# One more block of an MLP by fewer products: seven for block one's down projection, eleven for block two's up projection, with the weights' sums moved between engines

## The chip, the core and the metric

The kernel runs on one core of a Trainium2 chip. A core has five engines that work beside each other, each through its own queue in order: PE (TensorE, matrix products; the profile lists its weight loads apart as PEld), DVE (VectorE), ACT (ScalarE), POOL (GpSimd) and SP (SyncE, which issues most of the DMAs here). They meet only through semaphores. The metric is the time of one execution on the device in microseconds. Three executions before the change took 661.83, 662.26 and 664.05 us; the median is 662.26.

## What is computed

Two stages in float32. The first is a delta-rule attention over 4 batches, 8 heads, 768 tokens and head size 48. The second is an MLP over its output, 3072 tokens of 384 features, with 2048 hidden features. `_attn_ref` gets its shapes from q, k, v of (4, 8, 768, 48).

```python
for t in range(S):
    kt, vt, bt = (k_n[:, :, t], v[:, :, t], beta[:, :, t, None])
    y[:, :, t] = np.einsum('bhd,bhde->bhe', q[:, :, t], state)
    v_old = np.einsum('bhde,bhd->bhe', state, kt)
    state = state + bt[:, :, :, None] * np.einsum('bhd,bhe->bhde', kt, vt - v_old)
...
h = x @ w_in                       # x: (3072, 384), w_in: (384, 2048)
relu6 = np.clip(h + 3.0, 0.0, 6.0)
g = h * relu6 / 6.0
return (g @ w_out).astype(np.float32)   # w_out: (2048, 384)
```

`k_n` is k divided by its norm.

## The kernel before the change

**Tiling.** The 768 tokens are cut into 24 steps `t` of 32 tokens; with 4 batches one step is 128 rows. Two steps make a block of 256 rows, so the MLP has 12 blocks. The attention of a step is a chain of small products on PE: `sc` (scores, L547), `ks` (state times keys and queries, L806), `pz` (the inverse X times R, L827), `su` (the update of the state, L938), `py` and the transposition `yt`. X comes from an inverse of 32x32 triangles, done for a group of four steps at once: a transposition (L469), some sixty short steps on DVE that take turns (L759 multiplies into `pr`, L764 subtracts from `A`), and a transposition back (L473). The group that holds steps 5 to 8 is called `i2` in the order.

**The MLP of a block.** The up projection makes `ph`, ACT and DVE turn it into `g` (the hardswish), and the down projection multiplies `g` with `w_out` into `po`. There are two forms of each:

- the plain up projection `up` (L994): for each of 16 chunks f three products of 128x256, then ACT's relu (L1001) and a DVE step (L1004) that reads `ph` and so releases its place in PSUM;
- `up_by_eleven`: the product as blocks of 2 by 2 with sums taken on both sides. It needs sums of `w_in` (`S1`, `S2`, `S4` and a changed `W21`, made by `weight_sums` on POOL at L1030, 16 operations of 128x256), sums of the tokens (`token_sums`, DVE L1056), and per pair of chunks two sums on POOL (L1030), two on DVE (L1093, L1097), ACT's L1080, L1100 and L1110 and DVE's L1113;
- the plain down projection `down` (L1162): for each of the two steps 16 products of 128x384, then an eviction on ACT (L1173) and a DMA;
- `down_by_seven` (L1226): seven products of halves, 8 matmuls of 128x192 each. It needs sums of `w_out` (`T1`, `T2`, `T4`, and a changed quarter `B12`), made by `quarters` (L1197, 12 operations of 128x384 on DVE) and `last_quarter` (L1203, 4 more), and per block eight sums of `g` on DVE (L1212), five copies on ACT (L1233) and seven adds of results on POOL and DVE (L1236).

`FIRST = 2` says that block two's down projection is the first by seven, `UF = 3` that block three's up projection is the first by eleven. Blocks zero and one are plain, and so is block two's up projection.

**Where things lie.** `T1`, `T2` and `T4` live in the three parts of `spare`. Parts 0 and 1 hold raw data of weight pieces before they are converted, part 2 holds scratch of the conversion. The conversion of a piece is three steps on DVE (L378, L383, L389, the word `c` in the order) and four on ACT (L356, the word `a`). The last piece, number 15, lies raw in part 1. `S1`, `S2`, `S4` live in `sums_in`, which serves as scratch of the attention early on. All small products share PSUM: `po`, `ph`, `pt`, `py`, `yt` and `pz` take turns in four places (the ring `pm`), `sc`, `ks` and `su` in two (the ring `pc`). A place is taken again when its reader on DVE or ACT is done.

**What sets the order.** The first part of the program is written out by hand in `ORDER`: each word emits the next unit of one of several generators (`u` a unit of the MLP, `ru` a relu, `gu` the DVE step L1004, `i2` a step of the second inverse, `h4`, `y4`, `p8` and so on the attention's). `mlp_units` interleaves block zero's down projection with block one's up projection, 32 units of `u`, and then goes on to block one's down projection, four units of which are in `ORDER`. From step 5 on a loop of 15 units for each step takes over: it takes the attention's parts at fixed units (`plan`), one unit of the MLP, one of `rest` (the conversion, then `quarters`), and fills in the next inverse. `weight_sums` is taken two operations to a unit in block two's down projection. Each engine runs its instructions in the order in which they are emitted, and waits at each for what it needs.

## Time and profile before

| What | Value |
|---|---|
| executions | 661.83, 662.26, 664.05 us (median 662.26) |
| profiled execution: span from first to last instruction | 660.3 us |
| median less span | 2.0 us; no other time of the profiled execution is listed |
| granted TensorE clock, mean | 0.997 |
| block zero's down with block one's up projection | about 94 to 151 us |
| block one's down projection, plain | about 148 to 179 us |
| block two's up projection, plain | 178.8 to 205.9 us |
| block two's down projection, by seven | 205.9 to 230.2 us |
| block three's up projection, by eleven | 230.2 to 255.9 us |
| token step 5: `pz` on PE | 160.96 us |

How to read it: the profile has a row for each engine with its busy time; PE's matmuls overlap by pipelining, so the distance from one piece of the chain to the next is a better measure of PE work than the time of one record. Each fp32 matmul of the program appears as two records. A timeline row gives start, duration, engine, line, output and inputs; in brackets the idle time ahead of it and what ended it. A windows row gives the length of a stretch, the busy time of PE, PEld, DVE, ACT and POOL with the number of instructions, the granted clock and the DMA share with its rate. Line numbers are those of the kernel before.

### The profile page before, as it was taken

What the parts mean: (1) busy time and instruction counts of PE and PEld (TensorE: products, weight loads), DVE (VectorE), ACT (ScalarE), POOL (GpSimd) and SP (SyncE); (2) the same over time, 40 slices, a digit from 0 to 9 for tenths busy, and PEclk for the clock granted to TensorE, in tenths of its full rate; (3) what the DMA queues carried; (4) which work ended last, traced back from release to release, by engine and by line L of the source; (5) the groups of instructions that cost most, each with busy time, mean ns of one, the idle gap of its engine ahead of it and who ended that gap; (6) DMA issues with size and microseconds to landing.
All of it is one profiled execution on the core that took longest, in us unless ns stands there. A gap on an engine that the chain in (4) does not pass through costs nothing.

```text
span 660.3 us, 26640 instructions
## 1 busy us (share of the span) xinstructions
PE 632.5 (96%) x11640; PEld 569.2 (86%) x11640; DVE 499.2 (76%) x1170; ACT 282.3 (43%) x548; POOL 225.1 (34%) x352
## 2 busy tenths in 40 slices
PE   2768999999999999999999999999999999999997
PEld 2658987776689989999999999999999999999997
DVE  5899877798657988758988848979658998456354
ACT  5887689332243154154154244244244144153250
POOL 6531022003661353553254354164051242331430
PEclk9998999999999999999999999999999999999999
DMA  7888346202040030041030030020020020000000
GB/s 174 204 198 235 77 102 164 51 25 43 9 87 18 3 74 3 3 90 22 3 74 3 2 74 3 2 63 2 3 50 2 3 49 3 23 18 2 26 1 24
DMA packets 88692, 33.28 MB, mean 50 GB/s; under 512 B 80224, under 2 KB 83424, under 8 KB 88576
## 3 DMA queue, kind: packets, MB, share of 16 engines
q1 hardware_dynamic: 88224, 31.29, 20.8%
q8 instruction: 91, 1.49, 0.9%
q10 hardware_dynamic: 352, 0.30, 0.2%
q14 instruction: 25, 0.20, 0.1%
HBM read 26.84 MB, written 4.72 MB: 48 GB/s over the span
## 4 chain that ended last, share of the span: by engine, by line
PE 91%; DVE 3%; DMA 2%; SPq 1%; ACT 1%; issue 1%; DVEq 0%
PE po L1226 28%; PE ph L1066 27%; PE ph L994 9%; PE po L1162 6%; PE ks L806 4%; PE su L938 3%; PE pt L524 3%; PE pz L827 3%; PE py L827 3%; PE sc L547 2%; PE yt L873 1%; DMA spare<-in_moe_w_in_dram 1%; PE pi L684 1%; DMA w_out<-in_moe_w_in_dram 1%; SPq L168 1%
## 5 line engine op out<-in xcount | busy, mean ns | idle before, releaser
L1066 PE MATMUL ph<-xT,w_in 128*128 128x128 f32 (+1 forms) x720 | 156.8, 321 | 0.0
L1030 POOL TENSOR_TENSOR g<-g 128x256 f32<-128x256 f32 (+1 forms) x144 | 88.6, 616 | 104.7 <-ACT g L1080 99.1
L1066 PEld LDWEIGHTS ph<-xT,w_in 128*128 128x128 f32 x720 | 116.8, 191 | 6.7
L1226 PE MATMUL po<-w_out,g 128*128 128x192 f32 x640 | 110.6, 326 | 0.0
L1226 PEld LDWEIGHTS po<-w_out,g 128*128 128x128 f32 x640 | 104.6, 190 | 0.5
L1080 ACT ACTIVATE g<-ph 128x512 f32<-128x512 f32 x72 | 43.1, 598 | 105.1 <-PE ph L1066 105.1
L1226 PE MATMUL po<-spare,g 128*128 128x192 f32 x480 | 86.7, 332 | 0.0
L1226 PEld LDWEIGHTS po<-spare,g 128*128 128x128 f32 x480 | 77.2, 190 | 1.8
L994 PE MATMUL ph<-xT,w_in 128*128 128x128 f32 (+1 forms) x384 | 72.0, 338 | 0.6 <-ACT xT L877 0.6
L1236 POOL TENSOR_TENSOR o<-o,u 128x192 f32<-128x192 f32 x18 | 13.3, 739 | 163.8 <-ACT o L1233 86.6
L994 PEld LDWEIGHTS ph<-xT,w_in 128*128 128x128 f32 x384 | 59.6, 195 | 7.7 <-ACT xT L877 0.8
L1093 DVE TENSOR_TENSOR g<-ph,g 128x256 f32<-128x256 f32 x72 | 30.2, 419 | 46.8 <-PE ph L1066 33.5
L759 DVE TENSOR_TENSOR pr<-A 128x30 f32<-128x30 f32 (+9 forms) x150 | 57.3, 382 | 3.3
L1212 DVE TENSOR_TENSOR g<-g 128x512 f32<-128x512 f32 x80 | 56.1, 722 | 3.5 <-PE po L1226 3.5
L1113 DVE SCALAR_TENSOR_TENSOR g<-o,g 128x512 f32<-128x512 f32 x72 | 52.6, 730 | 7.8 <-ACT o L1110 7.7
L764 DVE TENSOR_TENSOR A<-A,pr 128x30 f32<-128x30 f32 (+9 forms) x150 | 55.1, 367 | 3.3
L1110 ACT ACTIVATE o<-g,halves 128x512 f32<-128x512 f32 x72 | 52.2, 725 | 11.3 <-DVE g L1113 8.4
L1066 PE MATMUL ph<-beta_tok,sums_in 128*128 128x128 f32 x288 | 55.9, 275 | 0.0
L356 ACT ACTIVATE spare<-spare,places 128x768 uint16<-128x768 uint16 (+1 forms) x56 | 52.8, 947 | 3.2 <-DMA kf<-in_k_dram 1.6
L1233 ACT ACTIVATE o<-po 128x192 f32<-128x192 f32 x40 | 13.3, 332 | 82.7 <-PE po L1226 79.2
L510 POOL TENSOR_TENSOR kb<-kf,inv 128x384 f32<-128x384 f32 x24 | 21.7, 907 | 75.5 <-issue 43.1
L1162 PE MATMUL po<-w_out,g 128*128 128x384 f32 x128 | 45.4, 490 | 0.0
(141 smaller groups left out, 1019.1 us busy)
## 6 DMA issues: line engine op xcount, KB each, us to landing
kf<-in_k_dram SPq DMA_DIRECT2D x96, 48.0 KB, 2.6
qb<-in_q_dram SPq DMA_DIRECT2D x96, 48.0 KB, 2.4
vf<-in_v_dram SPq DMA_DIRECT2D x96, 48.0 KB, 2.1
out_dram<-o SPq DMA_DIRECT2D x90, 48.0 KB, 1.6
spare<-in_moe_w_in_dram SPq DMA_DIRECT2D x4, 768.0 KB, 6.6
w_out<-in_moe_w_in_dram SPq DMA_DIRECT2D x4, 768.0 KB, 6.1
w_out<-in_moe_w_out_dram SPq DMA_DIRECT2D x4, 768.0 KB, 5.8
spare<-in_moe_w_out_dram SPq DMA_DIRECT2D x4, 768.0 KB, 5.2
```

Source lines behind the costliest of these rows:

```text
L356: nc.scalar.activation(out=z, in_=z if n else d.bitcast(I16)[:, :, :, 3], func=func, bias=places[:, n : n + 1], scale=scale,)
L759: nc.vector.tensor_tensor(out=pv, in0=A[:, j + 1 :, j].unsqueeze(2).to_broadcast([n, w, j]), in1=A[:, j, 0:j].unsqueeze(1).to_broadcast([n ...
L764: nc.vector.tensor_tensor(out=A[:, j + 1 :, 0:j], in0=A[:, j + 1 :, 0:j], in1=pv, op=ALU.subtract)
L994: nc.tensor.matmul(ph[:, cols], lhsT=w_in[:, s, f * 128 : (f + 1) * 128], rhs=xT[:, s, cols], start=(s == 0), stop=(s == NKT - 1),)
L1030: nc.gpsimd.tensor_tensor(out=out, in0=a, in1=b, op=op)
L1066: nc.tensor.matmul(ph[:, n], lhsT=w, rhs=x, start=start, stop=stop, skip_group_check=True)
L1080: nc.scalar.activation(out=gt, in_=ph[:], func=ACTF.Copy)
L1110: nc.scalar.activation(out=r, in_=g, func=ACTF.Relu, bias=half, scale=1.0 / 6.0)
L1113: nc.vector.scalar_tensor_tensor(out=g, in0=r, scalar=1.0, in1=g, op0=ALU.min, op1=ALU.mult)
L1162: nc.tensor.matmul(pos[c][:], lhsT=gs[blk, f // 2][:, f % 2, c * P : (c + 1) * P], rhs=w_out[:, f, :], start=(f == 0), stop=(f == NFC - 1),)
L1212: nc.vector.tensor_tensor(out=A(f, *out, 4), in0=A(f, *a, 4), in1=A(f, *b, 4), op=op)
L1226: nc.tensor.matmul(ps[n][:], lhsT=A(f - f % 2, *a)[:, f % 2], rhs=b[:, f], start=(f == 0), stop=(f == HF - 1),)
```

## The change

Four things change together.

1. `FIRST` goes from 2 to 1: block one's down projection is by seven products. For this block product 2 is done in four parts: two ahead of product 4, two behind it, and ahead of product 4 the program asserts that the sums of `w_out` and all hidden features are there. `settle()` at the start is left out for it.
2. `quarters` makes all sixteen sums of `w_out`, now on POOL, and `last_quarter` is gone. They are emitted by a new word `T` of the order, sixteen times, between the units of block zero's down and block one's up projection. The four that overwrite `B12` come last, behind block zero's products that read it. The second and third converting step of the last weight piece and its last step on ACT are emitted earlier, so that they stand ahead of the sums that read them.
3. `UF` goes from 3 to 2: block two's up projection is by eleven. `weight_sums` is taken in block one, one operation to a unit of its down projection (sixteen units) instead of two to a unit in block two's.
4. `rest` is the conversion alone, and the special cases for plain blocks behind block zero are gone.

```diff
 ORDER (its last lines)
-u h4 k*2 c q k*9 q u p8*2 x4 k ru k*2 gu k c n9 q u q*2 p8 k*2 b7 n9*2 i2 u x4 q i2*2 q ub ru gu u
-rb gb i2*2 h4*2 u*2 i2 ru i2*6 y4 i2 gu i2*7 u i2 ru gu i2 u*3 ru i2*4 gu ru i2*2 v i2 c gu u*3 a u
-ru c i2 u*2 i2 gu i2*3 q ...
+u h4 k*2 c q k*9 q u p8*2 x4 k ru k*2 gu k c a n9 q u T q*2 p8 k T k b7 n9 T n9 i2 c u T x4 q i2 c
+i2 q ub T ru gu u rb T gb i2*2 T h4*2 u T u i2 ru i2 T i2*4 T i2 y4 i2 gu T i2*4 T i2*3 u i2 T ru gu
+i2 u T u*2 ru i2*2 T i2*2 gu ru i2 T i2 v i2 gu u*4 ru i2 u*2 i2 gu i2*3 q ...
...
-    UF = 3
+    UF = 2
...
+        past.add(("down", c, f0))
...
-    FIRST = 2
+    FIRST = 1
...
     def quarters():
-        for o, a, b in ((T1, B12, B11), (T2, B22, T1), (T4, T2, B21)):
+        for o, a, b, hi in (
+            (T1, B12, B11, False), (T2, B22, T1, True), (T4, T2, B21, True), (B12, B22, B12, True),
+        ):
             for f in range(0, HF, 2):
-                nc.vector.tensor_tensor(
+                needs(("w", NWI + (f + HF * hi) // WF), ("w", NW - 2 + hi))
+                if o is B12:
+                    needs(("down", 0, f), ("down", 1, f))
+                nc.gpsimd.tensor_tensor(
                     out=o[:, f : f + 2], in0=a[:, f : f + 2], in1=b[:, f : f + 2], op=ALU.subtract
                 )
+                if o is B12 and f == HF - 2:
+                    past.add("quarters")
                 yield
-
-    def last_quarter(f):
-        nc.vector.tensor_tensor(
-            out=B12[:, f : f + 2], in0=B22[:, f : f + 2], in1=B12[:, f : f + 2], op=ALU.subtract
-        )
...
-        def product(n, a, b, half):
+        def product(n, a, b, part, parts=2):
...
-            for f in range(half * HF // 2, (half + 1) * HF // 2):
+            for f in range(part * HF // parts, (part + 1) * HF // parts):
...
-        settle()
+        if blk > FIRST:
+            settle()
         product(1, A11, B11, 0)
...
+        parts = 2
+        if blk == FIRST:
+            parts = 4
+            for part in range(2):
+                product(2, A12, B21, part, parts)
+                yield
+            needs("quarters", *(("read", ("ph", blk, f, None)) for f in range(NFC)))
         product(4, A22, T4, 0)
...
-        product(2, A12, B21, 0)
+        product(2, A12, B21, parts - 2, parts)
...
-        product(2, A12, B21, 1)
+        product(2, A12, B21, parts - 1, parts)
...
-            for _ in downs(blk):
-                next(sums, None)
+            for _ in down_by_seven(blk):
                 next(sums, None)
                 yield
             if blk + 1 < N // CB:
                 mode["of"] = "eleven" if blk + 1 >= UF else "up"
-                for n, _ in enumerate((up_by_eleven if blk + 1 >= UF else up)(blk + 1)):
-                    if blk + 1 == FIRST and n >= HF:
-                        drain(rest)
-                        if n % 2:
-                            last_quarter(n - HF - 1)
-                    yield
+                yield from (up_by_eleven if blk + 1 >= UF else up)(blk + 1)
...
-    rest = chained(convert(), quarters())
+    rest = convert()
...
-        ua=up(0, 0), ub=up(0, 1), u=mlp_units(),
+        ua=up(0, 0), ub=up(0, 1), u=mlp_units(), T=quarters(),
```

## The prediction

> **What bounds the kernel now.** I read the page's busy shares and its forty slices first, then the chain that ended last, then the windows between 94 and 256 us, and at last the timelines of VectorE (DVE) and GpSimd (POOL) in the stretch that the change touches.

> ```profile
> span 660.3 us, 26640 instructions
> PE 632.5 (96%) x11640; PEld 569.2 (86%) x11640; DVE 499.2 (76%) x1170; ACT 282.3 (43%) x548; POOL 225.1 (34%) x352
> PE   2768999999999999999999999999999999999997
> DVE  5899877798657988758988848979658998456354
> 119.00:154.00 35.00, 35.00 (x464) 25.35 (x464) 32.06 (x87) 9.86 (x22) 0.00 (x0) 1.00 0.21 43
> ```

> PE is full from 61 us to the end, so a microsecond of PE work is worth a microsecond wherever nothing else is late. The windows row (busy us of PE, PEld, DVE, ACT, POOL) shows something second: from 119 to 154 us DVE is busy for 32.06 of 35 us and POOL runs nothing. The next rows are of the chain, then of the timelines of DVE and of POOL.

> ```profile
> 154.80 1.49 PE po L1162 x4
> 205.86 2.60 PE po L1226 x16
> ```

> ```profile
> 124.07 1.95 DVE L469 STREAM_TRANSPOSE A<-L 128x1024 f32<-128x1024 f32 x1
> 127.44 0.25 DVE L759 TENSOR_TENSOR pr<-A 128x84 f32<-128x84 f32 x1
> 133.72 0.41 DVE L1004 SCALAR_TENSOR_TENSOR g<-g,ph 128x256 f32<-128x256 f32 x1
> 137.60 0.95 DVE L383 SCALAR_TENSOR_TENSOR spare<-spare 128x768 f32<-128x768 uint32 x1
> 159.10 0.60 DVE L909 SCALAR_TENSOR_TENSOR R<-ks,parity,R 128x384 f32<-128x384 f32 x1
> 173.03 2.35 DVE L1197 TENSOR_TENSOR spare<-spare,w_out 128x384 f32<-128x384 f32 x2
> 201.23 0.66 DVE L759 TENSOR_TENSOR pr<-A 128x84 f32<-128x84 f32 x1
> ```

> ```profile
> 154.89 0.83 POOL L510 TENSOR_TENSOR kb<-kf,inv 128x384 f32<-128x384 f32 x1 [43.06 <-issue]
> ...
> 173.03 0.83 POOL L498 TENSOR_TENSOR bkb<-kb,beta_tok 128x384 f32<-128x384 f32 x1
> 173.82 1.14 POOL L510 TENSOR_TENSOR kb<-kf,inv 128x384 f32<-128x384 f32 x1
> ...
> 201.06 0.73 POOL L1030 TENSOR_TENSOR sums_in<-sums_in,w_in 128x256 f32<-128x256 f32 x1
> 216.26 0.59 POOL L1236 TENSOR_TENSOR o<-o,u 128x192 f32<-128x192 f32 x1 [13.68 <-ACT o L1233]
> ```

> DVE shows no idle gap from 121.65 to 162.74: it runs the inverse of the second group (L469, then L759/L764 in turn), which token 5's pz needs together with R, finished at 159.70. PE starts that pz at 160.96, so this chain has 1.26 us to spare, and it has POOL silent beside it (43.06 us idle). That silence matters: the same L759 step takes 0.25 us at 127.44 and 0.66 at 201.23, where a POOL operation of 0.73 began 0.17 us earlier. At 173.03 two L1197 that take about 0.55 each alone take 2.35 beside two POOL operations, and the second of these takes 1.14 instead of 0.83. Each waits for the other in turn. Steps that read PSUM (L1004, L956) keep their time beside POOL.

> **The change, part by part.**

> *PE work.* Block one's product: 64 records of L1162, pieces of the chain 2.58+2.58+1.49+1.29+2.58+1.49+1.29+2.78+2.78+1.29+1.29 = 21.44 us. By seven it is 112 records like block two's, 2.60+1.50+1.30+2.60+5.40+2.80+2.60 = 18.80: -2.64. Block two's up projection: 96 records of L994, 4.08+1.49+1.30+2.59+5.38+2.79+3.89 = 21.52; by eleven like block three's, 3.38+1.09+1.54+2.43+2.62+2.62+2.62+3.96 = 20.26: -1.26. Together -3.90. Of the seven products three come before token 5's pz, where half of the old product stood, so PE would reach pz 2.6 us sooner; only the 1.26 lies behind it.

> *Sixteen sums from DVE to POOL in block zero.* DVE loses 12 L1197 and 4 L1203. Two of these stood before token 5's R (0.78 and 0.61 between starts): -1.39 there; one new L1212 takes their place, +0.60. In the built order the first T2 write needs the second converting step (L383) of the last weight piece to be done with that buffer; that step now stands behind the transpose, 124.07+1.95+0.95, about 127 us. The four T1 need only the piece before, and start near 115, beside PSUM steps and a 1.7 us gap: 0, at most 2 us. The other twelve, and the first four weight sums queued behind them (0.73 each), wait for nothing but their own queue, so sixteen POOL operations run from 127 on beside the L759/L764 chain.

> Price of one: POOL rows with two full inputs take 0.47 (128 columns), 0.59 (192), 0.73 (256); 0.27 more for 128 more gives 1.00 for 384, an estimate; the 0.83 row, whose second input is broadcast, is the lower bound. From the 173.03 rows: the first L1197 must have run from 173.72, 0.14 before POOL's end, and POOL's second from 174.13, 0.14 before DVE's end. So a POOL operation and a chain step of 0.25 take (1.00-0.14)+(0.25-0.14) = 0.97 us in turn, against 0.30 for the step alone: +0.67, twelve times 8.0. For the weight sums, with steps of 0.35, 0.59+0.21-0.40 = +0.40, four times 1.6. Five PSUM steps (three L1004, two L819, 0.33 apart) run in POOL's shadow: -1.6. The chain gets 8.0 us late (5.9 with 0.83; 10.2 if each holds for its whole length).

> [...]

> *How that reaches PE.* The last piece's two converting steps (0.95 each) move ahead of the chain, so the L1004 that release PSUM to PE before 137 are 1.9+8.0 = 9.9 late. The one at 133.72 ends 134.13; PE takes its slot at 134.61: 0.5 to spare, so PE stops 9.4. Its next outputs come 9.4 late, and DVE, only 8.0 late after the old place of these steps, waits for them: the chain is then 9.4 late too. The new product 4 takes a slot that L1004 (old end 154.36) releases: 163.8. From there to pz PE has 1.30+0.44+1.30+0.44+1.30 = 4.8: 168.6 against 160.96, +7.6; R, at 159.70-1.39+0.60+9.4 = 168.3, is in time.

> *Twelve weight sums and five output adds on POOL in block one.* They leave block two (where POOL idles 13.68 and 9.0 us) and go between kb, mb, bkb and sq, which fill POOL from 163.64 to 174.96 already. From the first kb (at 164.2 now: 154.76, where its norms end, +9.4) to the end of the second sq POOL has 3x0.83 (kb, kb, bkb), 4x0.61 (mb), 7x0.73 (weight sums), 0.59 (an add) and 2x0.82 (sq) = 12.3 us; with six waits of 0.45 for L1212, 15.0. DVE waits for that sq, sums it (0.55) and makes token 7's LB (0.75), whose PSUM slot PE's su needs: LB ends at 177.8 or 180.5, su is reached at 168.6+8.9 = 177.5. PE waits 0.3 to 3.0; I take 2.5, nearer to the upper, as the waits at 173.03 are of the same kind. Queued behind are two more sq and a kb that PE's pt needs: 0.7 more (0 to 1).

> *At no cost.* Behind R, seven L1212 (0.68) stand where ten L1197 stood. Block two's up projection gives DVE 8x(0.42+0.29+0.73) and 2.0 of token sums for 16x0.42 and 2.8 of L1203, +4.0 on 16.1 of 23 us; ACT +5 on 8.7; POOL 8x1.2 for 14 weight sums. Block three runs so at 21.65 of 26; without that cover 2 us. SP issues the same sixteen output DMAs for blocks zero and one; block one's wait for POOL's adds, with loads behind them that a later token needs.

> *Sum.* +7.6 -1.26 +2.5 +0.7 = +9.5. The profiled execution has a span of 660.3, and the median of the runs shown is 662.26, 2.0 more, around the span: 669.8 of span, 671.8.

> **The rivals.**

> A: *the POOL sums are hidden* (faster). They take place in 43 us of POOL idle time, and if they did not hold DVE, PE would win 1.7 at pz (154.4+4.8 = 159.2 instead of 160.96, product 4 still waiting for L1004) and 1.26 after: 659.3. It decides where a POOL operation costs the chain under about 0.15 us. Against it: 201.23 and 173.03, each 0.4 to 0.6.

> [...] From 231.77 to 235.74 five POOL operations lengthen four chain steps by 1.19 us, 0.24 each; sixteen give 3.8. pz then moves by 3.8-1.7 = +2.1, and with -1.26 and the 3.2 of block one the time is 666.3. Against it: there POOL waited for ACT between, and two PSUM steps lay beside it; the new ones queue back to back.

> C: *the two costs and the gain cancel*: lag of B, and block two's emptier POOL and DVE make up the waits of block one: +2.1-1.26, 663.1. PE has nothing to make up with after 61 us, which speaks against it.

> D: *POOL's queue in block one is worse*: its adds wait for ACT with all else behind them, block two's first g sums start late: 3 us more, 674.8. For it: 23 us of POOL work in some 25.

> **How the numbers follow.** My forecast 0.70, B 0.14, D 0.06, C 0.05, A 0.05. The range reaches from B to past D, 665.5 to 676.5; it takes in 5.9 and 10.2 us of lag, and leaves out A and C. Within 0.3% (2.0 us, about what a measurement can tell from no change) lies C: same 0.05, faster 0.05, slower 0.90.

> **What would show it.** In the changed profile: POOL busy from 127 to 139 us with sums of about 1 us each (0.83 would give some 2 us less); L759/L764 there near 0.9 us instead of 0.25; PE idle of 3 to 5 us twice before L994, released by DVE L1004; token 5's pz near 169; PE waiting before su, behind LB, near 178; block one's seven products 18.8 us of PE work. If L759 keeps 0.25 beside POOL, A holds and my main term is wrong; if POOL's sums run before 124 us, the term falls away too.

## The result, and the profile after

The changed kernel takes 678.97 us (median of 4 runs, 675.57 to 682.34) against 662.05 us (661.06 to 664.05) for the kernel before in the same comparison: 1.0246 times as long, with a 95% interval of 1.0206 to 1.0286. The prediction was 671.8, with a range of 665.5 to 676.5. The direction held; the loss is 16.9 us and not 9.5, and it lies outside the range.

The profiled execution has a span of 677.2 us, 16.9 more than the 660.3 of before. From the page of the changed kernel:

```profile
span 677.2 us, 26913 instructions
PE 635.2 (94%) x11736; PEld 579.8 (86%) x11736; DVE 511.0 (75%) x1176; ACT 286.1 (42%) x559; POOL 254.7 (38%) x389
PE   2769999869899998999999999999999999999997
POOL 6431213541975053363244354155042051241330
PEclk9978999969999998999999999999999999999999
```

TensorE (PE) is no longer full from 61 us on: its ninth slice falls to 6 and three others to 8, and its granted clock dips to 6 tenths at the ninth. The digits of GpSimd (POOL) show where its new work lies. The row of the windows for the stretch in question (busy us of PE, PEld, DVE, ACT, POOL, then granted clock, DMA share, GB/s):

```profile
119.00:154.00 35.00, 26.97 (x278) 19.08 (x277) 29.87 (x54) 6.21 (x14) 15.73 (x17) 0.85 0.09 17
```

PE loses 8.03 of the 35 us that it had filled before, GpSimd goes from 0 to 15.73 us, and the mean granted clock is 0.85. The timelines of GpSimd and of VectorE (DVE) show the cause side by side (start, duration, engine, line; `x4` means four operations in one row):

```profile
126.99 4.48 POOL L1204 TENSOR_TENSOR spare<-w_out,spare 128x384 f32<-128x384 f32 x4 [7.68 <-DVE pr L760]
131.43 3.91 POOL L1204 TENSOR_TENSOR spare<-spare,w_out 128x384 f32<-128x384 f32 x4
135.31 4.09 POOL L1204 TENSOR_TENSOR w_out<-w_out 128x384 f32<-128x384 f32 x4
```

```profile
130.63 0.94 DVE L760 TENSOR_TENSOR pr<-A 128x84 f32<-128x84 f32 x1
131.61 0.93 DVE L765 TENSOR_TENSOR A<-A,pr 128x84 f32<-128x84 f32 x1
...
135.53 0.97 DVE L765 TENSOR_TENSOR A<-A,pr 128x130 f32<-128x130 f32 x1
136.54 0.98 DVE L760 TENSOR_TENSOR pr<-A 128x150 f32<-128x150 f32 x1
```

The same L760 step of 128x84 took 0.25 us in the kernel before; beside a sum of 0.98 to 1.12 us it takes 0.94, and the next step starts 0.98 us after it instead of 0.28. One step of VectorE for each sum of GpSimd, in turn: that is the prediction's main step, with its size (0.97 us for a pair). So these two engines do not meet through semaphores alone, as the section on the chip has it. The timeline of PE, with its idle time before a row in brackets and what ended it:

```profile
129.03 0.88 PE L828 MATMUL pz<-R,X 32*32 32x48 f32 x64 [1.84 <-DVE g L1005]
138.93 2.92 PE L995 MATMUL ph<-xT,w_in 128*128 128x256 f32 x6 [3.65 <-DVE g L1005]
144.41 2.93 PE L995 MATMUL ph<-xT,w_in 128*128 128x256 f32 x6 [2.55 <-DVE g L1005]
166.09 1.54 PE L1230 MATMUL po<-spare,g 128*128 128x192 f32 x8 [0.61 <-DVE A L765]
171.05 0.88 PE L828 MATMUL pz<-R,X 32*32 32x48 f32 x64
182.19 0.84 PE L939 MATMUL su<-R,bkb 32*64 32x48 f32 x60 [1.97 <-DVE LB L559]
259.85 0.80 PE L828 MATMUL py<-R,LB 32*32 32x48 f32 x56
262.85 0.29 PE L828 MATMUL py<-R,LB 32*32 32x48 f32 x8 [2.20 <-issue]
309.00 0.27 PE L548 MATMUL sc<-KQ 64*32 64x64 f32 x2 [1.01 <-issue]
```

The stalls before L995 that L1005 ends, and the wait before su that LB ends, are those that were predicted. Two things were not. The L995 of six records take 2.9 us after the stalls, about twice what six take at full clock (1.46 us in a run below). And in block two PE stops twice in the middle of a group for 2.20 and 1.01 us with no semaphore to wait for ("issue"); the kernel before has no such row behind 61 us. The windows at those places give the clock:

```profile
137.60:147.90 10.30, 6.42 (x14) 4.47 (x15) 9.85 (x23) 0.95 (x2) 4.81 (x6) 0.50 0.00 1
263.90:267.30 3.40, 3.40 (x14) 2.93 (x14) 0.79 (x2) 1.49 (x3) 1.18 (x2) 0.50 0.02 5
```

Half clock for 10.3 us, beginning 2.3 us into the stall of 3.65 us, and again for 3.4 us, beginning 1.05 us after the gap of 2.20. The two rows agree in size (0.50, for one and for three times 3.4 us); what sets off the fall, and what sets its length, was not shown.

To compare kernels I use three stretches of PE, from the starts of token 1's, token 5's, token 8's and token 23's pz in the timelines. They leave out the start of the program, which differs by a microsecond or two from execution to execution.

| us | pz(1) to pz(5) | pz(5) to pz(8) | pz(8) to pz(23) | median time |
|---|---|---|---|---|
| before | 96.01 | 79.52 | 365.95 | 662.05 |
| changed | 106.44 | 81.14 | 371.15 | 678.97 |
| difference | +10.43 | +1.62 | +5.20 | +16.92 |
| predicted | +7.6 | +1.9 (2.5+0.7-1.26) | 0 | +9.5 |

The stretches are those of the one execution that was profiled; up to token 1's pz it is 0.3 us ahead of that of before. Of the 7.4 us between the loss predicted and the loss measured, 5.2 lie behind block one, where the prediction had put nothing, and 2.8 in block zero; block one gave 0.3 back, and the start another 0.3.

### The profile page after: what moved, and what is told of

Read it like the earlier page. It is cut to its first block, busy times and chain, and to the rows that moved or that the text cites. A ratio compares the mean times of both kernels' runs of the same rounds, so it can differ in the third digit from the quotient of the medians.

```text
span 677.2 us, 26913 instructions
## 1 busy us (share of the span) xinstructions
PE 635.2 (94%) x11736; PEld 579.8 (86%) x11736; DVE 511.0 (75%) x1176; ACT 286.1 (42%) x559; POOL 254.7 (38%) x389
## 3 DMA queue, kind: packets, MB, share of 16 engines
q8 instruction: 92, 1.51, 0.9%
## 4 chain that ended last, share of the span: by engine, by line
PE 83%; DVE 6%; POOL 3%; ACT 2%; SPq 2%; DMA 2%; issue 2%; POOLq 0%; DVEq 0%
PE ph L1067 29%; PE po L1230 28%; PE ph L995 5%; PE ks L807 3%; PE py L828 3%; PE su L939 3%; PE pt L525 3%; PE pz L828 3%; PE sc L548 2%; PE po L1163 2%; DVE A L765 2%; DVE pr L760 2%; ACT spare L357 2%; PE yt L874 1%; SPq L169 1%
## 5 line engine op out<-in xcount | busy, mean ns | idle before, releaser
L1031 POOL TENSOR_TENSOR g<-g 128x256 f32<-128x256 f32 (+1 forms) x160 | 97.7, 612 | 121.6 <-ACT g L1081 115.3
L1230 PE MATMUL po<-w_out,g 128*128 128x192 f32 x704 | 122.2, 326 | 0.1
L1230 PEld LDWEIGHTS po<-w_out,g 128*128 128x128 f32 x704 | 114.9, 190 | 1.0 <-ACT u L1237 0.3
L1230 PE MATMUL po<-spare,g 128*128 128x192 f32 x528 | 95.6, 332 | 0.6 <-DVE A L765 0.6
L1230 PEld LDWEIGHTS po<-spare,g 128*128 128x128 f32 x528 | 84.9, 190 | 2.7 <-issue 0.7
L1114 DVE SCALAR_TENSOR_TENSOR g<-o,g 128x512 f32<-128x512 f32 x80 | 58.7, 734 | 9.3 <-ACT o L1111 9.3
L760 DVE TENSOR_TENSOR pr<-A 128x30 f32<-128x30 f32 (+9 forms) x150 | 62.6, 417 | 3.6
L1216 DVE TENSOR_TENSOR g<-g 128x512 f32<-128x512 f32 x88 | 63.3, 739 | 2.5 <-PE po L1230 2.4
L1111 ACT ACTIVATE o<-g,halves 128x512 f32<-128x512 f32 x80 | 57.8, 723 | 12.5 <-DVE g L1114 9.4
L1067 PE MATMUL ph<-beta_tok,sums_in 128*128 128x128 f32 x320 | 62.1, 276 | 0.0
L995 PE MATMUL ph<-xT,w_in 128*128 128x128 f32 (+1 forms) x288 | 53.5, 337 | 7.0 <-DVE g L1005 6.2
L765 DVE TENSOR_TENSOR A<-A,pr 128x30 f32<-128x30 f32 (+9 forms) x150 | 57.7, 385 | 3.1
L995 PEld LDWEIGHTS ph<-xT,w_in 128*128 128x128 f32 x288 | 44.0, 205 | 13.3 <-DVE g L1005 7.5
L1067 PEld LDWEIGHTS ph<-beta_tok,sums_in 128*128 128x128 f32 x320 | 48.7, 192 | 0.0
```

The source lines that it names most:

```text
L760: nc.vector.tensor_tensor(out=pv, in0=A[:, j + 1 :, j].unsqueeze(2).to_broadcast([n, w, j]), in1=A[:, j, 0:j].unsqueeze(1).to_broadcast([n ...
L765: nc.vector.tensor_tensor(out=A[:, j + 1 :, 0:j], in0=A[:, j + 1 :, 0:j], in1=pv, op=ALU.subtract)
L995: nc.tensor.matmul(ph[:, cols], lhsT=w_in[:, s, f * 128 : (f + 1) * 128], rhs=xT[:, s, cols], start=(s == 0), stop=(s == NKT - 1),)
L1031: nc.gpsimd.tensor_tensor(out=out, in0=a, in1=b, op=op)
L1067: nc.tensor.matmul(ph[:, n], lhsT=w, rhs=x, start=start, stop=stop, skip_group_check=True)
L1111: nc.scalar.activation(out=r, in_=g, func=ACTF.Relu, bias=half, scale=1.0 / 6.0)
```

## The experiments

My theory after the result: the sums on GpSimd make block zero late (some 8 us) by taking turns with VectorE; the stalls halve PE's clock, which adds some; the queue of GpSimd in block one adds 2; and the late gaps are something else. The rivals: the moved order, the seven products' own waits, or block one's queue make most of the loss; and the late gaps belong to the eleven products.

The figures of every experiment in one table; what each is stands below. Each kernel's time is a median, with the ratio to the kernel before run beside it and its 95% interval; the stretches are of one execution. In most kernels it lies within about 2 us of the median; in "eleven only" it is the slowest of ten (666.43), in "sums on VectorE" the fastest of four (668.73), in "changed, shifted by 40" the fastest of six (687.90).

| kernel | time | ratio (95%) | pz(1)-pz(5) | pz(5)-pz(8) | pz(8)-pz(23) |
|---|---|---|---|---|---|
| seven only | 673.41 | 1.0163 (1.0134-1.0191) | 106.51 | 79.92 | 366.63 |
| eleven only | 664.15 | 1.0030 (1.0015-1.0046) | 96.22 | 80.26 | 370.03 |
| sums only | 673.66 | 1.0177 (1.0157-1.0197) | 107.43 | 79.52 | 365.79 |
| converts early | 663.95 | 1.0029 (1.0007-1.0051) | 97.40 | 79.52 | 366.13 |
| sums of w_out tiny | 669.08 | 1.0108 (1.0069-1.0147) | 98.39 | 82.50 | 366.88 |
| all sums tiny | 667.42 | 1.0062 (1.0040-1.0084) | 97.36 | 79.60 | 370.19 |
| sums on VectorE | 673.74 | 1.0181 (1.0131-1.0231) | 101.94 | 81.14 | 366.87 |
| stalls filled | 678.23 | 1.0234 (1.0196-1.0272) | 105.15 | 83.35 | 367.81 |
| changed, shifted by 40 | 691.19 | 1.0408 (1.0384-1.0433) | 113.15 | 81.15 | 367.02 |
| before, shifted by 40 | 675.46 | 1.0179 (1.0158-1.0200) | 103.12 | 79.93 | 366.87 |
| before, shifted by 64 | 663.96 | 1.0011 (0.9991-1.0031) | 97.20 | 79.51 | 365.73 |
| changed, 16 more | 676.96 | 1.0212 (1.0181-1.0243) | 108.42 | 81.60 | 366.25 |
| copies | 667.17 | 1.0046 (1.0024-1.0069) | 99.41 | 79.52 | 365.74 |
| fills too early | 665.91 | 1.0023 (1.0008-1.0039) | 99.16 | 79.53 | 366.08 |
| fills beside | 663.60 | 1.0008 (0.9989-1.0028) | 97.04 | 79.51 | 365.72 |

### Seven only

```diff
-    UF = 2
+    UF = 3
...
+                next(sums, None)
                 next(sums, None)
```

> The changed kernel with block two's up projection by six plain products and the fourteen to sixteen weight sums back in block two, two to a unit: block one alone is by seven products, with the sums of w_out on GpSimd in block zero as in the changed kernel. Theory 1 (GpSimd's sums hold VectorE's inverse chain in block zero, and that is the greater part of the loss): block zero stays as late as in the changed kernel (token 5's pz near 171 us against 160.96 before); the weight sums leave block one's GpSimd queue, so PE's wait before su (1.86 us) and about 0.7 more go, and block two's eleven products are lost again (+1.3): 677.7 us, 676 to 679. Rival 2 (the queue of GpSimd in block one is what cost the time): the kernel wins back 5 us or more, 674 or less, and su follows without a wait. Rival 3 (the gaps of 2.2 and 1.0 us late in the changed kernel, in which PE waited for nothing that the profile shows, belong to the eleven products of block two): they are gone, and the time is 674 to 676 although pz stands at 171.

Measured 673.41 us, 5.6 less than the changed kernel and less than theory 1 allowed; by the time, and by su without a wait, this is what rival 2 had forecast. The stretches say otherwise: block one gave back 1.2 us, and the late gaps the rest (+0.7 here in the last stretch instead of +5.2; one gap of 0.74 us near 480 is left). Block zero stayed as late (106.51). That is rival 3 in kind, 0.6 us below its band, but its reason was still to be tested: besides leaving out block two's eleven products, the kernel issues 96 records less on PE (48 of products and 48 of loads of weights).

### Eleven only

```diff
-    UF = 3
+    UF = 2
...
-                next(sums, None)
                 next(sums, None)
```

> The kernel before with only the second half of the change: block two's up projection by eleven products, and the weight sums on GpSimd in block one, one to a unit; block one is by plain products, the sums of w_out stay on VectorE. Theory 1 (the loss is made in block zero): pz of token 5 stays within 0.5 us of 160.96; PE saves 1.26 us in block two and may wait up to 2 us before su in block one, where the weight sums share GpSimd with kb, bkb and sq: 661 to 663.5 us. Rival 2 (the loss is made by the weight sums in block one): 665 us or more, with waits of PE before su and pt. Rival 3 (late gaps of PE of 1 us and more that no semaphore ends belong to the eleven products): such gaps stand in block two here too, and the time is 664 to 667 though pz and su are on time.

Measured 664.15 us, 0.3% slower than before, just above theory 1's band and at the foot of rival 3's. Block zero is on time (96.22). No wait before su appeared; one before yt did, on VectorE's y. And there is an issue gap again, as rival 3 had it, though at another place than in the changed kernel. From the timeline of PE:

```profile
201.59 0.52 PE L873 MATMUL yt<-ident,y 128*128 128x128 f32 x3 [1.32 <-DVE y L863]
269.33 0.27 PE L547 MATMUL sc<-KQ 64*32 64x64 f32 x2 [1.53 <-issue]
```

The clock was 0.5 for 3.4 us behind the second. The last stretch is 4.1 us longer than before. So eleven products alone win nothing: without its two waits (1.32 us before yt and 0.17 before a pt) the second stretch is 78.77 us against 79.52, a gain of 0.75 and not the 1.26 predicted, and the yt wait eats it. In the profiled execution, the slowest of ten, the late gap then makes it a loss; how much of it the others had isn't shown.

### Sums only, and converts early

Block zero alone, with and without the sums on GpSimd. The first:

```diff
-        for o, a, b in ((T1, B12, B11), (T2, B22, T1), (T4, T2, B21)):
+        for o, a, b, hi in (
+            (T1, B12, B11, False), (T2, B22, T1, True), (T4, T2, B21, True), (T4, T2, B21, True),
+        ):
...
-                nc.vector.tensor_tensor(
+                nc.gpsimd.tensor_tensor(
```

> Block zero as in the changed kernel, the rest as before: the converting steps moved ahead and sixteen sums of 128x384 on GpSimd beside the inverse chain (T1, T2, T4 and, so that the number is the same, T4 once more; the fourth quarter of w_out stays on VectorE in block two), blocks one and two by plain products. Theory 1: the L759 and L764 steps take 0.9 us beside the sums as in the changed kernel, PE stops twice for about 6 us together, pz of token 5 stands at 169 to 171 us, and nothing gives it back: 670 to 674 us. Rival 2 (the seven products' own waits in block one and the moved order, not the sums, made pz late): pz at 161 to 165, 662 to 667 us.

The second takes from the changed order only the words `a`, `c`, `c`, `c`:

```diff
-u h4 k*2 c q k*9 q u p8*2 x4 k ru k*2 gu k c n9 q u q*2 p8 k*2 b7 n9*2 i2 u x4 q i2*2 q ub ru gu u
+u h4 k*2 c q k*9 q u p8*2 x4 k ru k*2 gu k c a n9 q u q*2 p8 k k b7 n9 n9 i2 c u x4 q i2 c
```

> The kernel before with only the last scale step and three converting steps moved ahead to where the changed kernel has them, and the sums of w_out on VectorE behind them in their old places: no sum on GpSimd, no new products. Theory 1 (the moved steps cost only the lag of 1.9 us that they put on the first L1004 steps, of which 0.5 is to spare): 662 to 664 us, PE waits at most 1.5 us near 134, and the granted clock does not fall. Rival 2 (the moved order is what cost the time in block zero): pz of token 5 at 168 us or later, 668 us or more.

Measured 673.66 and 663.95 us. The first stretch is 107.43 and 97.40 us: the moved steps cost 1.4 there and the sums on GpSimd 10.0 more; behind that both kernels run as before (79.52 in both). The times are those of theory 1, and rival 2 of both fails. The sums on GpSimd alone are six tenths of the loss (10.0 of 16.9 us), and nothing later gives it back.

### Sums made tiny

```diff
-                    out=o[:, f : f + 2], in0=a[:, f : f + 2], in1=b[:, f : f + 2], op=ALU.subtract
+                    out=o[:, f : f + 2, 0:4], in0=a[:, f : f + 2, 0:4], in1=b[:, f : f + 2, 0:4],
...
-        product(4, A22, T4, 0)
+        product(4, A22, B21, 0)
```

> The changed kernel with the sixteen sums of w_out cut to 2x4 elements each (this leaves nearly all of these sums out; the products read unsummed quarters of w_out in their place, in the same sizes and number). Everything else is as in the changed kernel: converting steps moved, weight sums one to a unit on GpSimd in block one, seven products in block one and eleven in block two. Theory 1 (GpSimd's long sums hold VectorE's chain step by step): L759/L764's steps are back at 0.25 to 0.45 us, the granted clock stays at 1.0 around 138, token 5's pz stands at 160 to 163 us, and the time falls by the 10 us of block zero and some 2 us of the lowered clock: 664 to 669 us, the rest being block one's queue and the late gaps. Rival 2 (it is the number of GpSimd's operations or the moved order, not their length): 674 us or more.

This kernel leaves out nearly all of the sums of w_out. Measured 669.08 us, at the upper edge of theory 1's band: 9.9 less than the changed kernel for the length of sixteen operations alone, so rival 2 fails. The first stretch is 98.39, 8.05 us shorter than in the changed kernel, the lowered clock near 138 included, which is gone too. With nearly all of the weight sums left out as well:

```diff
-            plus_minus(S1[:, r], W21[:, r], W22[:, r], ALU.add)
+            plus_minus(S1[:, j, 0:4], W21[:, j, 0:4], W22[:, j, 0:4], ALU.add)
```

> As the kernel with tiny sums of w_out, and the sixteen weight sums of w_in cut to four columns as well (nearly all of both kinds of sums are left out; the products read unsummed weights of the same size). Theory 1: what block one loses by its GpSimd queue goes too: no wait of PE before su, 2 to 3 us less than with tiny sums of w_out alone; what then still stands against the arithmetic (660 us would be the kernel before less 2.64 and less 1.26, with the seven products' places) is the late gaps of PE: 660 to 665 us. Rival 2 (the weight sums cost nothing): the same time as with tiny sums of w_out alone, within 1 us.

Measured 667.42 us, above theory 1's band. The second stretch falls from 82.50 to 79.60: weight sums in block one cost 2.9 us here; PE's wait before su goes from 1.97 to 0.60 us, and half a clock from 175.7 to 179.1 behind that wait, about 1.7 us, goes with it. The changed kernel has the wait but not this lowered clock; against its 81.14 the weight sums cost 1.5 us. But the last stretch is 370.19 again, with issue gaps of 1.93 us at 252 and 0.94 at 296, where the kernel with full weight sums had one of 0.94. Both kernels issue the same records on PE in the same order, so such a gap hangs on the timing of the execution too, and not on the stream alone. The eight times of this kernel fall into two groups, 664.73 to 665.42 and 667.41 to 668.61; they are some 3 us apart, about what the gaps of 1.93 and 0.94 us of the profiled execution (667.44) make together (2.87), though only one execution was profiled and the cause of the two groups is not shown. And even with no sum to wait for, the change does not beat the kernel before: seven products save about 2.1 us of PE's work (its pieces take 19.3 us in the changed profile, where 21.44 stood), but in front of token 5's pz, where PE waits for VectorE anyway (97.36, as with the converts alone).

### Sums on VectorE

```diff
-                nc.gpsimd.tensor_tensor(
+                nc.vector.tensor_tensor(
```

> The changed kernel with the sixteen sums of w_out on VectorE, at the same places in the program. Theory 1 (the sums cost the chain because the two engines take turns, so their place on GpSimd gains nothing): twelve sums of about 0.6 us stand in VectorE's own queue, 7.2 us, against 8 to 10 on GpSimd; the L759/L764 steps are 0.25 to 0.45 us; pz of token 5 at 168 to 171 and the time 676 to 679 us. Rival 2 (GpSimd's idle time does cover part of the work): slower than the changed kernel by 3 us or more.

Measured 673.74 us (668.73 to 677.25), below theory 1's band, and rival 2 fails: on VectorE the same sums cost no more, and by the medians 5.2 us less, though the intervals of the two ratios just overlap and the profiled execution is the fastest. In that one the first stretch is 101.94 against 106.44: the sums add 4.5 us when VectorE does them itself (over the 97.40 of the converts) and 9.0 when GpSimd does. (Its last stretch is 4.3 us shorter because the gap of 2.20 us is missing there, though PE's stream is that of the changed kernel.) From VectorE's timeline in this kernel:

```profile
133.48 0.55 DVE L1204 TENSOR_TENSOR spare<-spare,w_out 128x384 f32<-128x384 f32 x1
133.95 0.31 DVE L760 TENSOR_TENSOR pr<-A 128x150 f32<-128x150 f32 x1
134.17 0.74 DVE L820 SCALAR_TENSOR_TENSOR y<-ks,parity,y 128x192 f32<-128x192 f32 x2
```

A sum occupies 0.47 us from its start to the next step's, while the same sum on GpSimd costs the chain 0.70 (0.98 from step to step instead of 0.28). The 43 us of idle GpSimd were no cover.

### The stalls filled with products

```diff
+                for _ in range({10: 14, 11: 9}.get(f, 0)):
+                    nc.tensor.matmul(
+                        wide[0][:, DM : DM + P], lhsT=w_in[:, 0, 0:P], rhs=xT[:, 0, 0:P],
+                        start=False, stop=False, skip_group_check=True,
+                    )
```

> The changed kernel, all its work kept, with 14 and 9 extra products of 128x128 on TensorE (0.22 us each) ahead of the tenth and eleventh outputs of block one's up projection, into unused columns of a PSUM tile: they fill most of the two stalls of 3.65 and 2.55 us and hold nothing up. Theory 1 (the stalls themselves lower the granted clock to 0.5 for some 10 us, and that is a cost of its own): the clock stays at 1.0 from 127 to 155 us, the L995 of six records after the stalls take 1.3 instead of 2.9 us, and token 5's pz comes 1 to 2 us sooner: 675 to 678 us. Rival 2 (what PE loses by the clock is hidden behind VectorE's chain, which sets pz): clock 1.0 but pz unmoved, time within 1 us of the changed kernel's 679. Theory 3 (the late gaps of PE hang on how its instructions fall on the fetches of 16 KB that the trace shows): the extra products shift everything behind them, so the gap of 2.2 us near 261 moves or goes, whatever pz does.

Measured 678.23 us. The clock between 137.6 and 147.9 is 1.00 now (0.5 is left from 132.0 to 135.4, behind the wait of 1.84 us before token 4's pz; twelve records of L1003 take 4.54 us there, and 2.86 in the changed kernel), and the plain up products behind the stalls, L1003 in this kernel, are short again:

```profile
138.78 3.29 PE L997 MATMUL po<-xT,w_in 128*128 128x128 f32 x28
141.90 1.46 PE L1003 MATMUL ph<-xT,w_in 128*128 128x256 f32 x6
143.20 2.17 PE L997 MATMUL po<-xT,w_in 128*128 128x128 f32 x18
146.41 1.56 PE L1003 MATMUL ph<-xT,w_in 128*128 128x256 f32 x6 [1.04 <-DVE g L1013]
```

The first stretch is 1.3 us shorter (105.15): what the halved clock behind the stalls costs block zero, at the lower end of theory 1. The time hardly moved, because the gaps moved, as theory 3 had it: the gap at 261 is gone, the last stretch is 367.81 instead of 371.15, and two new gaps stand in block one:

```profile
174.73 0.38 PE L548 MATMUL sc<-KQ 64*32 64x64 f32 x18 [1.85 <-issue]
186.97 2.38 PE L1239 MATMUL po<-spare,g 128*128 128x192 f32 x13 [1.63 <-issue]
```

### PE's stream shifted

This asks about the gaps by themselves: forty products of 32x16, placed where PE waits 8 us for its first operand, in both kernels.

```diff
             pt = psM.tile([128, NP, P], FP32, name="pt", tag=slot["pm"])
+            if t == 0 and j == 0:
+                for _ in range(40):
+                    nc.tensor.matmul(
+                        pt[0:32, 0, 0:16], lhsT=ident[0:32, 0:32], rhs=ident[0:32, 0:16],
+                        start=True, stop=True,
+                    )
```

> The changed kernel with forty extra products of 32x16 on TensorE at its very start, where TensorE waits 8 us for its first operand: no work and no wait behind them differs, only the place of every later instruction of TensorE in its stream (by 160 records and loads of weights). Theory 1 (the gaps of 2.2 us near 261 and 1.0 us near 308, which no semaphore ends, hang on how dense runs of small products meet the fetches of 16 KB on the instruction queue): the gaps move to other places or go, while the stalls at 129, 139 and 144 us and the wait before su stay; time 674 to 681 us. Rival 2 (they belong to the eleven products of block two and its data): the gaps stay at py near 261 and sc near 308, 679 us within 1.5.

> The kernel before with the same forty extra products at the start. Theory 1 (fetches): the kernel before shows no gap of PE behind 61 us because its stream happens to fall well; shifted, it shows gaps of 0.5 to 2 us in sc, py, pz or po that no semaphore ends, and takes 662.5 to 667 us. Rival 2: no gap, 662 us within 1.

Measured 691.19 and 675.46 us, with 664.13 for the kernel before beside them: 11.3 us more than before, and 10 to 12 more than the changed kernel, far beyond theory 1's bands. The extra products end at 6.40 us, and PE's next row starts at 8.23 us, where it stood before (8.08). From the timeline of PE, and the windows, of the kernel before with the shift:

```profile
52.91 0.86 PE L833 MATMUL py<-R,LB 32*32 32x48 f32 x32 [6.60 <-issue]
...
89.06 0.82 PE L944 MATMUL su<-R,bkb 32*64 32x48 f32 x57 [1.15 <-issue]
107.39 0.38 PE L833 MATMUL py<-R,LB 32*32 32x48 f32 x7 [2.31 <-issue]
```

```profile
46.00:53.00 7.00, 0.40 (x35) 0.27 (x25) 6.48 (x20) 2.54 (x3) 2.26 (x5) 0.74 1.04 326
```

PE stands still for 6.60 us in the middle of one group, in a stretch in which the DMA engines are full (share 1.04, 326 GB/s; the packet for instructions that lands before PE goes on starts only 3.8 us after PE stopped), and for 0.50 to 2.31 us at four other places before 110 us. In the shifted changed kernel both late gaps of block two are gone (last stretch 367.02, with one of 1.12 us near 494) while the stalls and the su wait stay.

The page of the changed kernel counts 92 fetches for instructions on queue 8:

```profile
q8 instruction: 92, 1.51, 0.9%
```

1.51 MB in 92 fetches are 16.4 KB each, and 11736 products and as many loads of weights are 255 records to a fetch; in the kernel before, 2 x 11640 = 23280 records in 91 fetches are 256 (the 23470 in the expectation below are the changed kernel's). If the place within a fetch matters, a shift by 256 records must do nothing. Forty products are 160 records (each makes two products and two loads); sixty-four are 256:

```diff
-                for _ in range(40):
+                for _ in range(64):
```

> The kernel before with sixty-four extra products of 32x16 at the start of TensorE's stream, in place of the forty that made it 12 us slower: 64 products are 256 records of TensorE (128 of products, 128 of loads), and the trace of the kernel before shows a fetch of 16 KB for every 256 records on average (23470 records, 91 fetches). Theory 1 (what counts is where instructions fall within a fetch): a shift by a whole fetch leaves every edge where it was, no gap of PE after 61 us, and the time is that of the kernel before plus the 1 us by which the products reach past the first wait: 662.5 to 665.5 us. Rival 2 (extra work at the start, or any shift of the stream, costs the 12 us): 673 us or more.

Measured 663.96 us, 1.0011 times the kernel before (0.9991 to 1.0031): more extra work than with forty, and the 11 us are gone. Rival 2 falls. Then the changed kernel, with sixteen such products in the stall before the tenth output:

```diff
+            if blk == 1 and f == 10:
+                for _ in range(16):
+                    nc.tensor.matmul(
+                        wide[0][0:32, DM : DM + 16], lhsT=w_in[0:32, 0, 0:32], rhs=xT[0:32, 0, 0:16],
+                        start=False, stop=False, skip_group_check=True,
+                    )
```

> The changed kernel with sixteen extra products of 32x16 ahead of the tenth output of block one's up projection, in the stall of 3.65 us, so that they cost no time there. Seven products for block one and eleven for block two add 48 products, 192 records; with the 16 the stream behind block two lies 256 records, a whole fetch, behind that of the kernel before. Theory 1 (fetch edges): no gap of 1 us or more that no semaphore ends in blocks two and three, where the changed kernel has 2.2 us with a lowered clock behind it and 1.0; what is left is block zero's and block one's loss: 672 to 676 us, unless the shifted part between 139 and 230 us has a gap of its own. Rival 2 (the late gaps have another cause): the gaps stay, 677 to 681 us.

Measured 676.96 us (675.42 to 679.79), a microsecond above theory 1's band. Behind 176 us there is no gap any more: the windows from 250 to 620 us, first of the changed kernel,

```profile
250.00:620.00 370.00, 366.71 (x6516) 342.19 (x6515) 283.94 (x654) 138.86 (x289) 135.48 (x203) 1.00 0.11 24
```

and then of this one:

```profile
250.00:620.00 370.00, 369.89 (x6564) 345.28 (x6566) 287.67 (x663) 140.69 (x294) 137.12 (x206) 1.00 0.12 24
```

PE idles 0.11 us there instead of 3.29, and the last stretch is 366.25, within 0.3 of the kernel before. In the whole time 2.0 us of this are left, and the intervals overlap, because the first stretch is 2.0 longer than in the changed kernel (108.42): 0.6 in two small issue gaps at 64 and 69 us, where the two streams are still the same, and 0.9 between token 4's and token 5's pz. The shift also makes a gap at a new place, as the expectation had left open; it costs little, since PE's wait before su falls from 1.97 to 0.34 us:

```profile
175.24 0.30 PE L548 MATMUL sc<-KQ 64*32 64x64 f32 x4 [1.66 <-issue]
```

So the eleven products do not cost the 5.2 us by their work or their waits. They move what follows against the fetches. All seventeen profiles bear this out. In eight of them (the kernel before, sums only, converts early, copies, both kernels with fills, before shifted by 64, and this one) the stream behind block two lies level with the kernel before or a whole 256 records behind it, and none of these has an issue gap of 0.4 us or more after 250 us. The nine others (28, 96, 160 or 192 records beyond a whole number of fetches) each have at least one.

The places can be counted too, as the number of PE's product records before each gap (the figure behind x): here for the two late gaps of the changed kernel, the second again in the kernel with all sums tiny, and for the gap near 107 in the kernel before shifted by 40 (windows of PE alone):

```profile
0.00:262.84 262.84, 225.26 (x5050) 0.95 0.40 92
0.00:308.99 308.99, 270.40 (x5810) 0.95 0.35 82
0.00:296.46 296.46, 264.79 (x5811) 0.98 0.37 85
0.00:107.38 107.38, 78.33 (x2384) 0.90 0.63 153
```

The 27 issue gaps of 0.4 us or more behind 61 us all fall on one grid, whichever the kernel: their counts lie within 5 of a grid of 127 product records to a step, which with their loads is a fetch of 16 KB (from 2384 to 5050 it is 21 steps, and from there to 5810 six). And in each of them PE goes on 1.23 to 1.57 us after a packet of queue 8 has landed. So these are waits for the next fetch at its edge. Where the stream lies is not all: with one and the same stream, the changed kernel, both kernels with tiny sums and the one with the sums on VectorE all have the gap at 5810 (0.94 to 1.01 us), but only two of the four have that at 5050.

### What of a GpSimd operation holds VectorE

Copies, with one input, in place of the sums; then fills, with none. The converting steps are moved as in "converts early" (97.40 in the first stretch) and the true sums stay on VectorE.

```diff
+        for a, hi in ((B11, False), (B22, True), (B21, True), (B12, True)):
+            for f in range(0, HF, 2):
...
+                nc.gpsimd.tensor_copy(out=T1[:, f : f + 2], in_=a[:, f : f + 2])
```

> The kernel before with the converting steps moved ahead as in the changed kernel (661.85 to 668.38, median 663.95, by itself) and sixteen copies of 128x384 on GpSimd beside the inverse chain, one input in place of two, into a place that VectorE overwrites later; the true sums stay on VectorE. Theory 1 (any GpSimd operation on the tiles takes turns with VectorE's steps of two inputs, for as long as it lasts): the L759/L764 steps beside a copy last as long as the copy, 0.5 to 0.9 us, and pz of token 5 is 4 to 9 us late: 668 to 673 us. Rival 2 (only sums with two full inputs hold VectorE): the steps stay at 0.25 to 0.45 us, and the time is 663 to 665 us.

Measured 667.17 us, just under theory 1's band. From the timelines of GpSimd and VectorE:

```profile
128.69 4.37 POOL L1198 COPY spare<-w_out 128x384 f32<-128x384 f32 x9 [6.98 <-DVE A L765]
```

```profile
129.79 0.44 DVE L760 TENSOR_TENSOR pr<-A 128x84 f32<-128x84 f32 x1
130.27 0.43 DVE L765 TENSOR_TENSOR A<-A,pr 128x84 f32<-128x84 f32 x1
```

A copy takes 0.49 us, and the step beside it 0.44 instead of 0.25: again one for one. Nine of the sixteen copies ran beside the chain. From token 4's pz to token 5's it takes 35.23 us instead of the 33.76 of the moved converts alone, 1.5 more (the rest of the 2.0 in the first stretch is mostly an issue gap of 0.61 us near 100). The chain's step lasts about as long as the GpSimd operation beside it. For fills, the first try told nothing, since they had run before the first L760 (the last ended at 122.35, L760 began at 127.83); its 99.16 us hold issue gaps of 0.47 and 0.49 us at 73 and 101:

```diff
-                nc.gpsimd.tensor_copy(out=T1[:, f : f + 2], in_=a[:, f : f + 2])
+                nc.gpsimd.memset(T1[:, f : f + 2], 0.0)
```

> The same with sixteen fills of 128x384 on GpSimd, which write and read nothing. Theory 1 (any GpSimd operation on the tiles takes turns with VectorE): steps of L759/L764 as long as a fill, pz of token 5 late by sixteen times what a fill lasts over a step, some 4 to 8 us: 667 to 672 us. Rival 2 (GpSimd's reading is what holds VectorE): steps at 0.25 to 0.45 us beside the fills, 663 to 665 us.

Held back by a small copy, twelve of them ran beside the chain:

```diff
+                if a is B22 and f == 0:
+                    nc.gpsimd.tensor_copy(out=T1[:, 0:2, 0:4], in_=B22[:, HF - 2 : HF, 0:4])
                 nc.gpsimd.memset(T1[:, f : f + 2], 0.0)
```

> As the kernel with sixteen fills (which ran before the chain began, and so told nothing of it), now with twelve fills of 128x384 on GpSimd held back by a copy of 2x4 elements that needs the last converted piece, so that they run beside L759/L764. Theory 1 (any GpSimd operation takes turns with VectorE): the steps of VectorE there last 0.4 us, as long as a fill, in place of 0.25, and pz of token 5 is 1 to 2.5 us later than without. Rival 2 (fills, which read nothing, do not hold VectorE): 0.25 to 0.32 us for the steps of 84 to 150 columns, as without GpSimd.

```profile
129.96 4.38 POOL L1203 MEMSET spare<- 128x384 f32 x12
```

```profile
130.64 0.24 DVE L760 TENSOR_TENSOR pr<-A 128x84 f32<-128x84 f32 x1
130.92 0.25 DVE L765 TENSOR_TENSOR A<-A,pr 128x84 f32<-128x84 f32 x1
```

0.24 and 0.25, as with GpSimd silent; 663.60 us, 97.04 in the first stretch, and 33.77 from token 4's pz to token 5's. Fills, which write but read nothing, do not hold VectorE here (0.24 and 0.25 us); copies, which also read, do (0.44).

## Why the prediction was wrong, step by step

*The sums and the chain: right, a little small.* Twelve pairs at 0.97 us and a chain 8.0 us late were predicted. The pairs took 0.95 to 1.01, and counted from token 1's pz the L765 of the first 240 columns starts 8.9 us later than the L764 of before (here the kernel before, then the changed one):

```profile
140.10 0.41 DVE L764 TENSOR_TENSOR A<-A,pr 128x240 f32<-128x240 f32 x1
148.65 0.41 DVE L765 TENSOR_TENSOR A<-A,pr 128x240 f32<-128x240 f32 x1
152.07 0.42 DVE L1005 SCALAR_TENSOR_TENSOR g<-g,ph 128x256 f32<-128x256 f32 x1 [3.01 <-ACT g L1002]
```

The steps that read PSUM kept their time beside the sums, as predicted: two L820 at 137.44 took 0.73 us together and L1005 at 138.47 took 0.41, as the two L819 (129.51) and the L1004 (133.72) of before did with GpSimd silent.

*How that reaches PE: right in kind, 2.8 too small.* Predicted +7.6 at token 5's pz, measured +10.43. The step that failed is "PE stops 9.4 ... the chain is then 9.4 late too": it let PE work at full speed between its stops. With a chain 8.0 late and outputs 9.4 late, VectorE would wait 1.4 us for them. It waited 3.01, for ACT's g, because from within the stall of 3.65 us on the clock was halved for 10.3 us and ACT's input came later. With the stalls filled with products the same wait is the predicted one:

```profile
152.39 0.42 DVE L1013 SCALAR_TENSOR_TENSOR g<-g,ph 128x256 f32<-128x256 f32 x1 [1.40 <-ACT g L1010]
```

So 1.6 of the 2.8 us are the halved clock, and 0.9 the longer chain (with the stalls filled the stretch is only 1.3 shorter, as the chain is another 0.3 later there). Product 4 started at 166.09 and not at 163.8, and from there to pz it took 4.96 us, with 4.8 predicted.

*The PE work: too hopeful.* -2.64 was about -2.1, and -1.26 was -0.75. The first lies in front of token 5's pz and bought nothing, as the sum had it.

*Block one's queue: right in kind, somewhat too dear.* +2.5 and +0.7 for the wait before su and what follows; the waits were 1.97 us before su and 0.17 before a pt. The second stretch grew by 1.62, which with the eleven's gain of 0.75 makes 2.4 for the queue and not 3.2. That the stretch came so near the predicted +1.9 is partly luck: the queue and the gain were both set too high.

*"At no cost": this is the step that failed most.* It costed block two and all behind it by busy times of VectorE, ACT and GpSimd, and there was no term for PE's instruction stream. 5.2 us were lost there: gaps of 2.20 and 1.01 us and half a clock for 3.4 us. They are waits for instruction fetches, at places set by where the stream lies against them. A shift by 160 records, at a place without cost, cost 11 us; a shift by 256 cost nothing that could be measured; and putting the changed stream back in step took the loss behind block two from 5.2 to 0.3 us. What stays open is why the fetch comes too late at one edge and in time at another, and at the same edge in one execution and not in the next: the trace shows when a packet ran, not what it waited for. Nor can the size of such a gap be worked out from the profile of before.

*The rivals.* A (sums hidden), B (0.24 us to an operation, 666.3 us) and C (with the lag of B, 663.1) fail at L760: 0.94 us and not 0.25 to 0.5. D (block one's queue worse) has the time that is nearest, 674.8, for a reason that did not happen.

## What to carry to other kernels

Before moving work from VectorE to an idle GpSimd, look at what VectorE does in that stretch: beside steps with two inputs in SBUF, each step here lasted about as long as the GpSimd sum beside it (0.93 to 0.98 us beside sums of 0.98 to 1.12), 0.70 us a sum against 0.47 when VectorE did the sum itself. Where PE is full, an edit that changes the number of its instructions also moves everything behind it against the fetches of 256 records, and can gain or lose microseconds (11 us here for 160 records, nothing that could be measured for 256) that have nothing to do with the edit. So when two variants differ by 1 or 2%, look for "issue" gaps on PE first, count PE's product records up to each of them, and compare again with the stream shifted by dummy products to the same place.
